# Attention and gated feed-forward on one core: batch 0's first layer and a third token tile of the second layer go from split to plain fp32 matmuls, in a new written-out order

## The chip, the core and the metric

The kernel runs on one core of a Trainium2 chip (trn2). The metric is the device time of one execution in microseconds, lower is better. The kernel before takes 394.97 us, the median of three runs (394.75 to 395.34).

## What is computed

Two blocks follow each other. The first is attention over a pack of 32 learned queries per head (8 batches, 8 heads, 576 tokens, 64 channels): the packed queries attend to k and v, and then q attends to the packed result. The second is a feed-forward block with a depthwise convolution of width 3 and a sigmoid gate.

```python
def sm_attn(qq, kk, vv):
    s = scale * np.matmul(qq, kk.transpose(0, 1, 3, 2))
    ...
    a = np.exp(s)
    a = a / (np.sum(a, axis=-1, keepdims=True) + 1e-09)
    return np.matmul(a, vv)
p_packed = sm_attn(p, k, v)
out = sm_attn(q, p_packed, p_packed)
...
h = np.maximum(x @ w_in, 0.0)
...
    conv_out += conv_w[k][None, None, :] * hp[:, k:k + S, :]
gate = 1.0 / (1.0 + np.exp(-conv_out))
return (h * gate @ w_out).astype(np.float32)
```

## The kernel before

**Tiling.** The attention runs in 16 groups of four heads, two groups for each batch. A group's softmax weights over the 32 packs end up transposed as a tile of 128 x 576 (`a2t`, line 940), that is 32 packs of four heads by 576 tokens. The packed values are not multiplied with these weights. They are folded into w_in first (`packed_weight`, lines 957 to 1018), so that the first layer of a batch is one product of the folded weights `gw` and the softmax weights `a2`.

**Split matmuls.** Both layers keep fp32 accuracy by splitting. An operand x becomes hi (a rounding cast to fp32r, a reduced format that TensorE takes in one go) and lo (x minus hi), and a product is three fp32r matmuls: hi with hi, lo with hi, hi with lo. For the softmax weights the cast is line 945 and the subtraction line 947. For the folded weights the cast is line 1006, and for batches 0 and 1 the remainder comes from TensorE, which subtracts hi from the bank with a matmul by minus the identity (line 1010), and a second cast (line 1015). For a tile of 128 tokens in front of the second layer these are `x` (line 1194) and `xl` (line 1201). The steps share the helper lines 334, 337, 342 and 344, so that in a profile one finds them by their tiles.

**First layer** (`ffn1`, line 1026). A batch has 8 chunks of 128 of the 1024 channels. Each is 12 matmuls of 288 columns (two groups, three products, two halves), then Relu, the three taps of the convolution, Tanh and the gate on ScalarE and VectorE.

**Second layer** (`ffn2`, line 1152). There are 36 tiles of 128 tokens. Each is 8 steps, and a step is three matmuls of 512 columns (line 1227). The first `F2F` tiles do without the split: a step is one plain fp32 matmul (line 1174) on w_out as loaded.

**What sets the order.** The kernel is a set of generators, one for each piece of work, and the string `ORDER` says by two characters at a time whose next step is emitted. Each engine works through its instructions in that order, and SyncE (SP) does the same with the loads. A planner in the same file (`Flow`) estimates when a TensorE step can start. As long as the second layer has not got to the tile behind those named in `SPLIT`, it puts matmuls on zeros (`warm`, line 288, here called fills) into gaps that it expects. They are real instructions of the program, whether the gap then is there or not.

**Switches.** `F1F` names batches whose first layer is plain fp32 (empty before), `F2F` the number of plain tiles of the second layer, `ON_DVE` and `ON_POOL` the steps that go to VectorE and GpSimd in place of their default engine.

```python
if g // NG in F1F:
    yield Step("DVE", 669, take=["a2"], give=["s2"], sets=[("hi", g), ("a2", g)])
    at = wk.tile([128, S], F32, name="a2f", tag="a2hi", bufs=4)
    nc.vector.transpose(out=at, in_=s2)
...
if b in F1F:
    ...
    copy(key, hi[:, :, n * p : n * p + n], t)
    gw[b, hf] = (hi,)
    continue
```

Of the kernel before, what the change touches and what calls it, by code (L numbers as in the profile page):

```python
# [18 lines left out]


ORDER = (
    "0036360336367f6y03026y36360736340504340501050a0504060a70060570346z053a0e05090805350c363405366z36340c0c34363b0505"
    "0d0h0h0572050c3b34050c7205053c050b0d05760l0b713b0j050c0c710j0c0c050j3d0c3b3q3q050c0c0k770c3d0c3d3q0o0o740k3q740g"
    "0c0c0i0j0c730i0j0c733d0c0q0c0q3e3f0q3q0f0c3q783s0j3g0r3q3f3f3s3s3s0j3f0j3i3q3t0m0n3h3k0j793s3h3h0j3t3s3t3u0j0r0q"
    "0j3u3s3j0q3t3h3r3t3j7a3v3r3v0q3u0p0q0p753r3j3u3j0q3v5y3t3u750q3v373r5z3l3t0s0q3w3v3m3u0j0q3r377b3w3l0j3u3l3w0q0j"
    "5z3w3x3l3r3j3x3r3v3r0j0q0v5y0j5z37403x3v0q0x3w3n0j5z5y400x0q400x3w0z3x7c3y0q5y3n403y3x0x3w3z3x3n0x3o0j0q0q0j3y12"
    "413z3n3x0j0t3p5y3y5y143p7d5z3y0u3p3z0q415z0q0x16143z0q143p3y413n3y3z3j425z5y413n3z3z424242435z3l155y440y60424314"
    "600y430x0x4244190w42433l445y3843603p601444456010434560154518115y43444544600x3p45464446465z45466045140x1461461b60"
    "46606061470x474748131b1d61461b0x49476161481b480x616149141g47616149471b6114484948140x481760494947484962140x4a6261"
    "4b1k0x0x1i4b631c1s1b0x611i1e621463621c3862141i1b621b621i1a0x1f621i0x1n381j1b624b0x621414621i1j1p1p1b6314634a1463"  # L30
    "1b146363631p631b63624a141i141p1b1i141q1r641h641l634c1u1b1y1p4c4c4d4d1i4e4d1b64641b4c1w4c4e1q1i4c4d4e4e4d1p4c641w"
    "4e1b4d1w644e65644d1b654f1p4f4g1i631p211m4g1b1w4f1p1w641o1i4k4k4g4f231p4e1w4f1p64644k4h4f4f4i641b251i1x4g4g1i1p4g"
    "651i4g1i6565651b1i1t1i2866656565234h4j1x4i4i4h651w1p23234j641w4l4j1w1v231i65661z391i244h2a1w23664i5z4j244i4j664h"
    "664j4j1w4l1p1i23664i664h2a2a6666231p4m1p4i4n4m661p4m4h67674l4o4n664m23681w4n1p2a4n6767674o2k6767671p67204m4n4o4m"
    "2a4m4p4o4n2c2b674p664n4q3967261w682a222f232b1w4q394p4o4u4q274q4o2a232j4o4q65692h2h694q2m1w681w4u1p4q4p68681w681p"
    "4r4p4r2h68684u682d68682i4s4p2h2a4s294r4s1w6969692a694p69232h4t4t2e68694t4s4r69694r2o1w4s4v4t6a6a2o692a2q2h1w6a2i"
    "4s4r6a2x2o4t4t4r6a6a4s4t236a2h2o6b2a236a6b1w2p236a6a69232h676a4w2o2a4x232t4w6b2h2a4w4y4v6c2p6b6b232l2g4w4w6b6b6b"
    "4y234w6b4x4w4z6b4x2v4z4y2z6b4y2a544v6c232h4x2o2v6d4y4z6c4x4x2v6c6a6c4z6c4z4x2h6c6c234y6c542v2h6c6d6c2h504y6b2a6d"
    "6e506d6d506d2h2a6d4z6d306d2r6e2w6c4z2n6d502w6d512v546f506e5051506e2o526e51516f2o516e6d6e53526e512h532o6e2a522a52"
    "6e2y532v32556e2h2a2h2o51522a6f2a6f52322h322v556f6f6f2o536e5356522o6f6f6f2h53565757536f6g58562v6g2o562h6g6g6g5758"  # L40
    "56576h576g6h566g562o6g586g6g58322o596g6h2o586h5755596h2s6i6g6h575a6h593258332v59585a5a6h6h59596i5a6h5b6j596h5a5a"
    "5b5c2o5c6i6i6j6i5b5a5d6i6i2o6i6h6i2h6i5d5c2u5b5e5c2v6i5f5b326j6j5b5d6j6j6j2o5e6f5d6j6j5c5d5d5c6i5b5e2o5d6j335f5c"
    "322v2o6k6k5g2v5f5h5g2v5g6j326k6l5i6k5h6k5i5g5h2v326k6k6k5h5h5h316k5i5h5j6k6k5g6l325j5i6k5j325o325j5j5j5i6l6l6l6l"
    "6l6l322v6l6m5j5o6m6l6l5i5g325k5k6j6n6m6m5o6m2v6m6m5g5k5i6m6m5l5l6m2v5m322v6n2v5k6m5k322v5l6n325k6n5k5m6n6m5m5l6n"
    "6o5n5m5m6o326n5n6n5n5n6n6l6n6n2v5l5l5p325n5n6o5m5l326o6n6o5n6o6o5m6p6o326o5p6o5q5q5r5s5r5p6o5q6p6p6p6p6p5q5r5q5s"
    "6p5q5s6q6p5q6p6p5t6q5s6p5t5s5r6q6q5t6r5s6o5t6q5r6q6q5t5s5r5t6q6q5u6r6q5t5r5u6s5u6q5v5w6r6r5u5v5u5u6r5u6r5w5v6s5w"
    "6r5v5w5x6r6p5x5v6r5w5x6r6s5w6s5v6r6s6s6s5x5x5x5w5v6s5x6s6t6s6t6t6u6r6t6t6s6t6t6t6u6t6t6u6u6s6v6v6t6u6u6u6u6u6u6w"
    "6v6v6v6t6v6u6v6v6w6v6v6q6w6u6w6w6w6w6v6w6w6w6x6x6x6x6v6x6x6x6x6x6x6w7e7e6x7e6w7e7e7e7e6x7e7e7e"
)


# [167 lines left out]
def tile_packed_attention_conv_gate(  # L219
# [79 lines left out]
    def early():  # L299
# [118 lines left out]
    def weight(i):  # L418
# [10 lines left out]
        if src.dtype != F32:  # L429
# [411 lines left out]
    def attention(g):  # L841
# [115 lines left out]
    def packed_weight(b, hf):  # L957
# [5 lines left out]
        for p in range(parts):  # L963
# [62 lines left out]
    def ffn1(b, j):  # L1026
# [125 lines left out]
    def ffn2(m):  # L1152
# [164 lines left out]
```

## Time and profile before

| what | value |
|---|---|
| median of 3 runs | 394.97 us |
| the profiled execution, its own time | 394.99 us |
| its span | 393.2 us |
| TensorE matmuls, busy | 386.5 us, 98% of the span |
| TensorE weight loads, busy | 310.8 us, 79% |
| VectorE | 334.5 us, 85% |
| ScalarE | 247.5 us, 63% |
| GpSimd | 72.6 us, 18% |
| mean granted clock of TensorE | 0.998 |

The span is the profiled part; 1.8 us of the execution's own time lie around it. A matmul's busy time holds its way through the array too, and neighbours overlap in it. What a matmul costs the engine is read from one start to the next. PE is TensorE, PEld its weight loads, DVE VectorE, ACT ScalarE, POOL GpSimd, SP SyncE. A plain fp32 matmul stands in the trace as two records, so that "x4" in a row of line 1174 is two steps.

### The profile page before, as it was taken

How to read it: one execution, taken by the hardware profiler on the slowest of the kernel's cores; microseconds unless marked ns; L12 is line 12 of the kernel's file. 1: busy time of each engine (PE TensorE's matmuls, PEld its weight loads, DVE VectorE, ACT ScalarE, POOL GpSimd, SP SyncE). 2: the span in 40 equal slices, each digit the busy share in tenths (PEclk: the TensorE clock that was granted, in tenths of full speed). 3: DMA queues.
4: the chain of work that ended last, by engine and by line, in shares of the span. 5: the costliest groups of instructions: out<-in, count | busy, mean ns of one | idle time of the engine just before them, and what ended most of it. 6: DMA issues, size and time to landing. Idle time of an engine off the chain costs nothing.

```text
span 393.2 us, 8191 instructions
## 1 busy us (share of the span) xinstructions
PE 386.5 (98%) x3300; PEld 310.8 (79%) x3300; DVE 334.5 (85%) x501; ACT 247.5 (63%) x405; POOL 72.6 (18%) x59
## 2 busy tenths in 40 slices
PE   8999999999999999999999999999999999999996
PEld 6667655789678787878797887888797879898886
DVE  4899999999989999999899989799988897987010
ACT  4799999987666776765746465564645555444211
POOL 2041134204441331052120103000001100200420
PEclk9999999999999999999999999999999999999999
DMA  8999799797499779578655134001001110000211
GB/s 268 367 374 363 161 263 156 144 187 147 99 175 168 127 171 152 120 149 162 129 81 140 43 87 88 1 28 53 28 2 53 41 41 27 28 0 28 80 54 56
DMA packets 157527, 47.63 MB, mean 121 GB/s; under 512 B 145444, under 2 KB 148772, under 8 KB 157488
## 3 DMA queue, kind: packets, MB, share of 16 engines
q1 hardware_dynamic: 157024, 45.89, 49.5%
q10 hardware_dynamic: 432, 1.18, 0.9%
q8 instruction: 26, 0.43, 0.5%
q14 instruction: 13, 0.11, 0.1%
q0 software_dynamic: 32, 0.02, 0.0%
HBM read 37.64 MB, written 9.44 MB: 120 GB/s over the span
## 4 chain that ended last, share of the span: by engine, by line
PE 89%; DMA 4%; DVE 3%; ACT 1%; issue 1%; SPq 1%; ACTq 0%; DVEq 0%
PE fo L1227 43%; PE big L1047 24%; PE sm L1227 4%; PE big L731 4%; PE big L1174 4%; PE big L982 3%; DMA hgt<-in_q_dram 3%; PE sm L876 2%; PE big L868 2%; DMA hgt<-in_k_dram 1%; PE fo L1133 1%; PE sm L1133 1%; ACT tmp L510 1%; PE big L711 0%; PE big L1010 0%
## 5 line engine op out<-in xcount | busy, mean ns | idle before, releaser
L1227 PE MATMUL fo<-wo_hi,xhi 128*128 128x512 f32 x240 | 96.5, 402 | 0.0
L1227 PE MATMUL fo<-wo_hi,xlo 128*128 128x512 f32 x240 | 94.0, 392 | 0.0
L1227 PE MATMUL fo<-wo_lo,xhi 128*128 128x512 f32 x240 | 93.6, 390 | 0.0
L1064 ACT ACTIVATE hbuf<-big 128x576 f32<-128x576 f32 x62 | 40.8, 659 | 52.7 <-PE big L1047 52.3
L1096 DVE SCALAR_TENSOR_TENSOR hgt<-hbuf,cw,hgt 128x576 f32<-128x576 f32 x64 | 53.4, 843 | 5.7 <-ACT hgt L1094 5.4
L1047 PE MATMUL big<-a2hi,ghi 128*128 128x288 f32 x256 | 57.0, 304 | 0.0
L1047 PE MATMUL big<-a2lo,ghi 128*128 128x288 f32 x256 | 54.9, 295 | 0.0
L1047 PE MATMUL big<-a2hi,glo 128*128 128x288 f32 x256 | 54.9, 295 | 0.0
L1227 PEld LDWEIGHTS fo<-wo_hi,xhi 128*128 128x128 f32 x240 | 45.0, 188 | 11.8 <-issue 0.9
L1104 ACT ACTIVATE hgt<-hgt 128x576 f32<-128x576 f32 x64 | 43.7, 693 | 16.6 <-DVE hgt L1100 16.5
L1227 PEld LDWEIGHTS fo<-wo_hi,xlo 128*128 128x128 f32 x240 | 45.0, 188 | 10.0
L1100 DVE SCALAR_TENSOR_TENSOR hgt<-hbuf,cw,hgt 128x576 f32<-128x576 f32 x64 | 51.2, 811 | 0.5
L1227 PEld LDWEIGHTS fo<-wo_lo,xhi 128*128 128x128 f32 x240 | 45.1, 188 | 7.4
L1106 DVE SCALAR_TENSOR_TENSOR hgt<-hgt,hbuf 128x576 f32<-128x576 f32 x64 | 47.5, 752 | 3.5 <-ACT hgt L1104 3.0
L1047 PEld LDWEIGHTS big<-a2hi,ghi 128*128 128x128 f32 x256 | 43.1, 189 | 6.9 <-issue 1.6
L337 POOL TENSOR_TENSOR xlo<-hgt,xhi 128x1024 fp32r<-128x1024 f32 x11 | 27.1, 2467 | 88.0 <-ACT xhi L344 57.2
L1047 PEld LDWEIGHTS big<-a2lo,ghi 128*128 128x128 f32 x256 | 41.1, 188 | 0.0
L1047 PEld LDWEIGHTS big<-a2hi,glo 128*128 128x128 f32 x256 | 41.0, 188 | 0.0
L1242 ACT COPY o<-fo 128x512 f32<-128x512 f32 x30 | 17.6, 585 | 34.8 <-PE fo L1227 26.8
L1094 ACT ACTIVATE hgt<-hbuf,cw 128x576 f32<-128x576 f32 x42 | 32.8, 788 | 2.6 <-DVE hbuf L1062 2.0
L344 ACT CAST xhi<-hgt 128x1024 fp32r<-128x1024 f32 (+1 forms) x29 | 27.6, 956 | 8.9 <-PE fo L1227 4.0
L337 POOL TENSOR_TENSOR s<-s,mx 128x576 f32<-128x576 f32 x10 | 13.0, 1300 | 100.0 <-DVE hgt L1100 67.2
(127 smaller groups left out, 593.4 us busy)
## 6 DMA issues: line engine op xcount, KB each, us to landing
out_dram<-o SPq DMA_DIRECT2D x35, 256.0 KB, 2.2
k<-in_k_dram SPq DMA_DIRECT2D x48, 144.0 KB, 3.3
q<-in_q_dram SPq DMA_DIRECT2D x48, 144.0 KB, 3.1
v<-in_v_dram SPq DMA_DIRECT2D x40, 128.0 KB, 3.0
v<-in_v_dram SPq DMA_DIRECT2D x6, 512.0 KB, 9.7
hgt<-in_moe_w_in_dram SPq DMA_DIRECT2D x3, 1024.0 KB, 12.0
hgt<-in_moe_w_out_dram SPq DMA_DIRECT2D x3, 1024.0 KB, 6.8
k<-in_k_dram SPq DMA_DIRECT2D x2, 576.0 KB, 10.5
```

The lines of the kernel that those rows point to most:

```text
L337: added = nc.gpsimd.tensor_tensor(**kw)
L344: nc.scalar.copy(out=out, in_=in_)
L731: nc.tensor.matmul(out=o.rearrange("c (j r) -> c j r", r=NR) if by_block(g) else o, lhsT=lhs[r, 32 * cols[i] : 32 * cols[i] + 32], rhs=rhs ...
L1047: nc.tensor.matmul(out=t[:, hf, :SH], lhsT=w[:, gg, js], rhs=x[:, hf * SH : (hf + 1) * SH], start=n == 0, stop=n == (1 if b in F1F else 3) ...
L1064: nc.scalar.activation(out=inner, in_=t[:, :, :SH], func=AF.Relu, scale=0.5)
L1094: nc.scalar.activation(out=d, in_=h[:, 1 : S + 1], func=AF.Copy, scale=cw[:, NJ + j : NJ + j + 1])
L1096: nc.vector.scalar_tensor_tensor(out=d, in0=h[:, 0:S], scalar=cw[:, j : j + 1], in1=d, op0=ALU.mult, op1=ALU.add)
L1100: nc.vector.scalar_tensor_tensor(out=d, in0=h[:, 2 : S + 2], scalar=cw[:, 2 * NJ + j : 2 * NJ + j + 1], in1=d, op0=ALU.mult, op1=ALU.add)
L1104: nc.scalar.activation(out=d, in_=d, func=AF.Tanh)
L1106: nc.vector.scalar_tensor_tensor(out=d, in0=d, scalar=1.0, in1=h[:, 1 : S + 1], op0=ALU.add, op1=ALU.mult)
L1227: nc.tensor.matmul(out=t, lhsT=x[:, c, :], rhs=w[:, c % 2, :], start=c + i == 0, stop=c == NJ - 1 and i == 2)
L1242: nc.scalar.copy(out=o, in_=t)
```

## The change

Batch 0 goes into `F1F` and `F2F` goes from 2 to 3. Batch 0's two groups then no longer cast and subtract their transposed softmax weights, its four folded weight pieces are only copied (no remainder, no matmul by minus the identity), and a chunk of its first layer is 4 plain fp32 matmuls of 288 columns in place of 12 split ones. Token tile 2 of the second layer is 8 plain matmuls in place of 24 split ones and needs no cast and no subtraction of its tokens. `ORDER` is new up to about a third of its length and the same behind it, and some steps have another engine.

```diff
 ORDER = (
-    "0036360336367f6y03026y36360736340504340501050a0504060a70060570346z053a0e05090805350c363405366z36340c0c34363b0505"
...
+    "00367f3603360e6y073602033634366y36050a0536360570060105700434340a0c063a05040h340c0h050c6z056z3472363605090508723b"
...
 )
...
-    ON_DVE = {"gh001", "gh510", "gl000", "hi0", "hi12", "kT10", "relu34", "relu76", "tap00", "tap02", "tap22", "tap40", ...
-    ON_POOL = {"add00", "add10", "add11", "add30", "add50", "add60", "add70", "lo0", "lo10", "lo11", "lo4", "lo6", "lo7", ...
+    ON_DVE = {"a1T1", "gh510", "hi12", "kT00", "kT10", "kT20", "relu34", "relu76", "tap01", "tap03", "tap21", "tap40", ...
+    ON_POOL = {"add01", "add10", "add31", "add40", "add41", "add50", "add51", "add60", "add70", "add71", "lo10", "lo11", "lo7", ...
     COLD = 7
-    F1F = ()
-    F2F = 2
+    F1F = (0,)
+    F2F = 3
```

Over the whole program TensorE loses 96 split matmuls of the first layer, 24 of the second, 8 matmuls by minus the identity and one fill (24 in place of 25), and gains 32 plain matmuls of 288 columns and 8 of 512. VectorE has as many instructions as before (503), ScalarE 7 fewer, GpSimd 3 fewer, SP as many. The last 1377 matmuls are the same, in the same order.

TensorE around the start of the first layer, before. `a2hi`, `a2lo`, `ghi` and `glo` are the split softmax weights and folded weights, `idle` a fill, line 982 the folding, line 1010 the matmul by minus the identity:

```order
L291 MATMUL idle<-zeros 128x512 x4
L982 MATMUL big<-w_in_sb,ppT 32x256 x8
L1047 MATMUL big<-a2hi,ghi 128x288 x2
L1047 MATMUL big<-a2lo,ghi 128x288 x2
L1047 MATMUL big<-a2hi,glo 128x288 x2
...
L876 MATMUL sm<-v_88,a1T 32x64 x20
L1010 MATMUL big<-ghi,minus 128x256 x2
```

The same place in the change. `a2f` and `gwf` are the unsplit operands:

```order
L711 MATMUL big<-ident,q 128x128 x9
L731 MATMUL big<-kT,pT 32x288 x8
L291 MATMUL idle<-zeros 128x512 x4
L1047 MATMUL big<-a2f,gwf 128x288 x8
L982 MATMUL big<-w_in_sb,ppT 32x256 x8
L876 MATMUL sm<-v_88,a1T 32x64 x20
```

The second folding now stands behind the first two chunks, and the matmuls by minus the identity are gone. Ahead of the first matmul of line 1047 everything else on TensorE is there as often as before, fills included (24).

SP at the start of the program, one piece of the difference. Lines 643 are loads of k and q (`hgt_75<-in_k_dram` is group 1's keys, `k<-in_k_dram` those of groups 2 and 3), 603 and 613 of v, 411 of weights:

```order
 L788 DMA stage<-in_p_dram 32x16x64
+L643 DMA k<-in_k_dram 128x1152
 L643 DMA hgt_75<-in_k_dram 128x1152
 L603 DMA v_88<-in_v_dram 128x4x256
 L613 DMA v_88<-in_v_dram 64x4x64
 L411 DMA hgt_76<-in_moe_w_in_dram 128x4x512
-L643 DMA k<-in_k_dram 128x1152
 L643 DMA hgt_75<-in_q_dram 128x1152
 L603 DMA v_89<-in_v_dram 128x4x256
 L613 DMA v_89<-in_v_dram 64x4x64
```

Group 2's keys now go ahead of group 1's; what is loaded up to group 1's values (`v_89`) is the same.

SP further on, another piece of the difference, around the third and fourth block of w_out:

```order
-L652 DMA k<-in_k_dram 32x36x32 x4
-L411 DMA hgt_76<-in_moe_w_out_dram 128x2x1024
-L652 DMA k<-in_k_dram 32x36x32 x4
+L652 DMA k<-in_k_dram 32x36x32 x8
 L411 DMA hgt_76<-in_moe_w_out_dram 128x2x1024
```

The third block of w_out now stands behind eight loads of keys, not four.

## Rows read from the trace of the kernel before

**Rows 1.** The page, parts 1 and 4: busy time by engine; the chain's shares.
```profile
PE 386.5 (98%) x3300; PEld 310.8 (79%) x3300; DVE 334.5 (85%) x501; ACT 247.5 (63%) x405; POOL 72.6 (18%) x59
...
PE 89%; DMA 4%; DVE 3%; ACT 1%; issue 1%; SPq 1%; ACTq 0%; DVEq 0%
```

**Rows 2.** Busy time in stretches of 10 us, granted clock, DMA share, GB/s.
```profile
20.00:30.00 10.00, 9.71 (x139) 6.25 (x127) 9.40 (x18) 9.26 (x17) 5.29 (x4) 1.00 1.06 372
30.00:40.00 10.00, 9.86 (x139) 7.61 (x138) 9.19 (x17) 10.00 (x17) 1.30 (x1) 1.00 1.06 352
40.00:50.00 10.00, 9.81 (x116) 6.52 (x115) 10.00 (x16) 10.00 (x18) 2.15 (x2) 1.00 0.79 179
50.00:60.00 10.00, 9.99 (x70) 5.35 (x68) 10.00 (x18) 10.00 (x16) 3.95 (x4) 1.00 1.06 247
```

**Rows 3.** Who waited, TensorE, whole span: us in total, times, longest.
```profile
PE big L711 <- DMA hgt<-in_k_dram: 0.6, 1, 0.6
PE big L711 <- DMA hgt<-in_q_dram: 0.6, 1, 0.6
PE big L711 <- ACT hbuf L1064: 0.2, 1, 0.2
```

**Rows 4.** Timeline of TensorE up to batch 0's first chunk: start, us, then the group.
```profile
20.20 0.77 PE L876 MATMUL sm<-v,a1T 128*32 128x64 f32 x40
...
24.40 0.50 PE L1010 MATMUL big<-ghi,minus 128*128 128x256 f32 x2
24.74 1.15 PE L711 MATMUL big<-ident,k 128*128 128x128 f32 x9
...
29.05 1.19 PE L291 MATMUL idle<-zeros 128*128 128x512 f32 x4
30.18 0.66 PE L982 MATMUL big<-w_in_sb,ppT 64*32 64x256 f32 x16
30.77 0.53 PE L1047 MATMUL big<-a2hi,ghi 128*128 128x288 f32 x2
...
32.55 0.77 PE L876 MATMUL sm<-v,a1T 128*32 128x64 f32 x40
```

**Rows 5.** Timeline of VectorE: group 1's last transpose, and its neighbours.
```profile
25.96 0.67 DVE L342 CAST glo<-big 128x512 fp32r<-128x512 f32 x1
...
28.70 0.78 DVE L940 STREAM_TRANSPOSE a2t<-s 128x576 f32<-128x576 f32 x1
...
30.21 0.76 DVE L334 TENSOR_TENSOR a2lo<-a2t,a2hi 128x576 fp32r<-128x576 f32 x1
```

**Rows 6.** Timeline of TensorE: starts of a split chunk and of split steps.
```profile
157.22 0.43 PE L1047 MATMUL big<-a2hi,ghi 128*128 128x288 f32 x2
...
158.82 0.40 PE L1227 MATMUL fo<-wo_hi,xhi 128*128 128x512 f32 x1
...
161.57 0.48 PE L1227 MATMUL fo<-wo_hi,xhi 128*128 128x512 f32 x1
...
166.45 0.43 PE L1047 MATMUL big<-a2hi,ghi 128*128 128x288 f32 x2
```

**Rows 7.** Timeline of TensorE: plain fp32 steps and a matmul by minus the identity.
```profile
51.21 0.40 PE L1010 MATMUL big<-ghi,minus 128*128 128x256 f32 x2
51.44 1.88 PE L1174 MATMUL big<-w,hgt 128*128 128x512 f32 x4
53.25 1.09 PE L982 MATMUL big<-w_in_sb,ppT 64*32 64x512 f32 x16
...
59.10 1.03 PE L1174 MATMUL big<-w,hgt 128*128 128x512 f32 x2
59.97 0.81 PE L868 MATMUL big<-ident,a 128*128 128x128 f32 x5
...
63.29 1.98 PE L1174 MATMUL big<-tmp,hgt 128*128 128x512 f32 x4
```

**Rows 8.** Timeline of SP's issues: the third block of w_out, then four loads of keys.
```profile
45.13 0.87 SPq L411 DMA_DIRECT2D hgt<-in_moe_w_out_dram  x1
46.10 6.37 SPq L652 DMA_DIRECT2D k<-in_k_dram  x4
```

More of the change, by code (lines that the diff above doesn't have):

```diff
@@ L21 @@
 ORDER = (
-    "0036360336367f6y03026y36360736340504340501050a0504060a70060570346z053a0e05090805350c363405366z36340c0c34363b0505"
[L23 to L46, printed above, removed]
@@ L47 @@
-    "6r5v5w5x6r6p5x5v6r5w5x6r6s5w6s5v6r6s6s6s5x5x5x5w5v6s5x6s6t6s6t6t6u6r6t6t6s6t6t6t6u6t6t6u6u6s6v6v6t6u6u6u6u6u6u6w"
-    "6v6v6v6t6v6u6v6v6w6v6v6q6w6u6w6w6w6w6v6w6w6w6x6x6x6x6v6x6x6x6x6x6x6w7e7e6x7e6w7e7e7e7e6x7e7e7e"
+    "00367f3603360e6y073602033634366y36050a0536360570060105700434340a0c063a05040h340c0h050c6z056z3472363605090508723b"
+    "0c34050d0l0j760c05340d0b05710b3c3b053b05050j0g71350c0c0c053b05050o0c0c0j0o0j0c3q0j3d0c740c0c050i740k0c0c733q0c0c"
+    "3e0q0c0i77733f3d3d783s3s0q3s0q3f0f3g3t0k3d3f3s0r3q0m3s3t3i3t3q0j3f0r0j0q3s0n0j3u3h0j0q3t793s0j373u0q3t3h3r3h0q3h"
@@ new lines @@
+    "3v3t0j0q3r3u3j3v0j3k0p3t0j757a750q3w0s3u0p3v3r403u3u3v3j3v3w3r0q3u3j3w3v3x0j40373l0q3v3j0j0q0j3w3y7b3l3x603y3w3x"
+    "40375y0q3w0v0z5z0j3w0j400x3l0x3m0t600q3z0j3l0x0j0x123y3z3z3n0q3y0x0q0j3z0y5y5y5y7c3n0q3o603y3z0q16413j3n140u1441"
+    "3z0x3y5z0y5z415z0q0q143z3x3p7d3n603x3x410q603p3y5z3j3x3p1019420x5y424342423l0x3l42184343435z4244141d60151443423p"
+    "5y430w154443453n445y4660450x14453n440x46451b11445y45605z4644454661443p17455z46460x611b1g600x460x471b4748495y6013"
+    "4748470x3p4714491e6149140x48471b1b49616138481449485z6161494761494861611b481c5y0x621c0x14141b621k61631i4a4b1i1b62"
@@ new lines @@
+    "0x63141b62621i1a1i62380x624a621i5z611r62141f621i1n4a381j14141b1j14621b0x140x1b141p631p63631i631b4b6363631l1p1m14"
+    "641p634b141i1q141u631b644c1b4c1h4d1i63644c4c1q1b4d4c1s4e4d4d4c644e4c4d1p64644e4d1y1p4e4e4e654d1w1i4f1b1b1i1w1w4f"
+    "1i644g1p4e4h1x4g1i1p1w65641o1x4f1i211i6464231w1p1b4h4f4f4g234k644f1p4f254h4h664g231b4h1i1w4k641b1w4k1i654g1i6265"
+    "4h4i6565654h23664g1w651p1t651i1z23654j281w651i1i1p1v4i664i4i4j664g4i231w1p4j4i2a1w4l2a2a664m4i1p4n4j4j654j1p6666"
+    "4m664j66664o4n1w4m666724671p2a244m68391p671p4n1p23674n674o2k23674l2a6767674m4l4m204m4o4n4p4o232c2b4n66674p4n4q67"
@@ new lines @@
+    "1w262a68391w222f232b4q394p4o4u4q274q4o2j4o234q2a692h2h694q2m1w684u1p4q4p6868681w1p4r4p4r1w2h68684u682d68682i4s4p"
+    "2h4s294r4s2a691w6969692a4p692h234t4t2e68694t4s4r69694r2o1w4s4v4t6a6a2o2a692q2h1w6a2i4s4r6a2x2o4t4t4r6a6a4s4t236a"
+    "2h2o6b2a236a6b1w2p236a6a69232h676a4w2o2a4x232t4w6b2h2a4w4y4v6c2p6b6b232l2g4w4w6b6b6b4y234w6b4x4w4z6b4x2v4z4y2z6b"
+    "4y2a544v6c232h4x2o2v6d4y4z6c4x4x2v6c6a6c4z6c4z4x2h6c6c234y6c542v2h6c6d6c2h504y6b2a6d6e506d6d506d2h2a6d4z6d306d2r"
+    "6e2w6c4z2n6d502w6d512v546f506e5051506e2o526e51516f2o516e6d6e53526e512h532o6e2a522a526e2y532v32556e2h2a2h2o51522a"
@@ new lines @@
+    "6f2a6f52322h322v556f6f6f2o536e5356522o6f6f6f2h53565757536f6g58562v6g2o562h6g6g6g575856576h576g6h566g562o6g586g6g"
+    "58322o596g6h2o586h5755596h2s6i6g6h575a6h593258332v59585a5a6h6h59596i5a6h5b6j596h5a5a5b5c2o5c6i6i6j6i5b5a5d6i6i2o"
+    "6i6h6i2h6i5d5c2u5b5e5c2v6i5f5b326j6j5b5d6j6j6j2o5e6f5d6j6j5c5d5d5c6i5b5e2o5d6j335f5c322v2o6k6k5g2v5f5h5g2v5g6j32"
+    "6k6l5i6k5h6k5i5g5h2v326k6k6k5h5h5h316k5i5h5j6k6k5g6l325j5i6k5j325o325j5j5j5i6l6l6l6l6l6l322v6l6m5j5o6m6l6l5i5g32"
+    "5k5k6j6n6m6m5o6m2v6m6m5g5k5i6m6m5l5l6m2v5m322v6n2v5k6m5k322v5l6n325k6n5k5m6n6m5m5l6n6o5n5m5m6o326n5n6n5n5n6n6l6n"
@@ L49 @@
+    "6n2v5l5l5p325n5n6o5m5l326o6n6o5n6o6o5m6p6o326o5p6o5q5q5r5s5r5p6o5q6p6p6p6p6p5q5r5q5s6p5q5s6q6p5q6p6p5t6q5s6p5t5s"
+    "5r6q6q5t6r5s6o5t6q5r6q6q5t5s5r5t6q6q5u6r6q5t5r5u6s5u6q5v5w6r6r5u5v5u5u6r5u6r5w5v6s5w6r5v5w5x6r6p5x5v6r5w5x6r6s5w"
+    "6s5v6r6s6s6s5x5x5x5w5v6s5x6s6t6s6t6t6u6r6t6t6s6t6t6t6u6t6t6u6u6s6v6v6t6u6u6u6u6u6u6w6v6v6v6t6v6u6v6v6w6v6v6q6w6u"
+    "6w6w6w6w6v6w6w6w6x6x6x6x6v6x6x6x6x6x6x6w7e7e6x7e6w7e7e7e7e6x7e7e7e"
 )
@@ L251, in tile_packed_attention_conv_gate @@
     PE_LO = 2
-    ON_DVE = {"gh001", "gh510", "gl000", "hi0", "hi12", "kT10", "relu34", "relu76", "tap00", "tap02", "tap22", "tap40", "tap41", "tap42", "tap44", "tap46", "tap53", "tap56", "tap57", "tap60", "tap61", "tap64", "tap65", "tap67", "tap70", "tap72", "tap73", "tap74", "tap75", "tap77", "x140", "x180", "x230", "x270", "x280", "x310", "x340", "x90"}
-    ON_POOL = {"add00", "add10", "add11", "add30", "add50", "add60", "add70", "lo0", "lo10", "lo11", "lo4", "lo6", "lo7", "mul10", "mul12", "mul14", "mul2", "mul3", "mul4", "mul5", "mul6", "mul7", "mul9", "sub10", "sub11", "sub15", "sub2", "sub3", "sub4", "sub5", "sub6", "sub8", "sub9", "xl100", "xl110", "xl20", "xl280", "xl30", "xl320", "xl330", "xl350", "xl50", "xl60", "xl70"}
+    ON_DVE = {"a1T1", "gh510", "hi12", "kT00", "kT10", "kT20", "relu34", "relu76", "tap01", "tap03", "tap21", "tap40", "tap41", "tap42", "tap44", "tap46", "tap53", "tap56", "tap57", "tap60", "tap61", "tap64", "tap65", "tap67", "tap70", "tap72", "tap73", "tap74", "tap75", "tap77", "x140", "x180", "x230", "x270", "x280", "x310", "x340", "x90"}
+    ON_POOL = {"add01", "add10", "add31", "add40", "add41", "add50", "add51", "add60", "add70", "add71", "lo10", "lo11", "lo7", "mul0", "mul10", "mul12", "mul14", "mul4", "mul5", "mul6", "mul9", "sub10", "sub11", "sub15", "sub3", "sub4", "sub5", "sub7", "sub8", "sub9", "xl100", "xl110", "xl280", "xl30", "xl320", "xl330", "xl350", "xl50", "xl60", "xl70", "xl80"}
     COLD = 7
-    F1F = ()
-    F2F = 2
+    F1F = (0,)
+    F2F = 3
     SPLIT = (0,1)
```

## The prediction

> **What bounds the kernel now.** I read the page first, then the stretches of 10 us, TensorE's waits, and then the timeline of TensorE from start to start. TensorE's matmuls cover 98% of the span, and the chain that ended last lies on it for 89% [rows 1]. That alone is weak, because fills count as busy and neighbouring matmuls overlap. The waits say more: besides the wait for the first memset, the profile knows three idle stretches of TensorE in the whole run, 0.6, 0.6 and 0.2 us [rows 3]. Fills cover most of what else was lost, and the program has 25 of them. All but one stand ahead of batch 0's first layer, which begins at 30.77 us [rows 4]. Behind that there is always real work for TensorE, at the full granted clock: it is busy 9.99 of 10 us from 50 to 60 us, while VectorE and ScalarE are busy for 10.00 of 10 as well [rows 2]. So I read two regimes. Up to about 30 us TensorE waits for loads and for the attention's chain over VectorE and ScalarE; from there to the end, the time is the sum of what TensorE has to do. The change removes work mostly from ScalarE and adds work to TensorE, and most of it lies in the second regime.
>
> **First layer of batch 0.** A split chunk in steady state runs from 157.22 to 158.82 us: 1.60 us for 12 matmuls [rows 6]. The chunk at the start took 1.78 us, 30.77 to 32.55, because it follows other kinds of matmul [rows 4]; the new chunks have the same neighbours, so I compare without that. A plain fp32 matmul of 288 columns is not in the trace. The nearest is one of 512 columns: 0.87 us (59.10 to 59.97), and 0.905 us as the mean of the two between 51.44 and 53.25 [rows 7]. By columns 288 take 0.49 to 0.51 us, so a chunk of four takes 1.96 to 2.04 us. The gain is then 0.36 to 0.44 us a chunk, or as little as 0.18 if the whole 1.78 us were the split chunk's own. I take 0.36, since the 0.905 includes a change of kind: 8 x 0.36 = **+2.9 us** (1.4 to 3.5).
>
> **Third token tile.** A split step costs 4.88 / 7 = 0.70 us (161.57 to 166.45, seven steps [rows 6]), a plain one 0.87 to 0.905 [rows 7]. 8 x 0.17 = **+1.4 us** (to 1.6).
>
> **Matmuls by minus the identity.** Four pairs go. One pair held TensorE from 24.40 to 24.74, 0.34 us [rows 4], another for 0.23 us, 51.21 to 51.44 [rows 7]. I take 0.34: **-1.4 us** (-0.9 to -1.4). **One fill fewer**: four took 1.13 us (29.05 to 30.18 [rows 4]), so **-0.3 us**.
>
> **Start of the first layer.** Ahead of its first matmul TensorE has the same work and the same 24 fills as before, except one folding of 0.59 us (30.18 to 30.77) and one of the pairs, 0.34 us [rows 4]. With the same lost time it starts at 30.77 - 0.93 = 29.84 us, and nothing is won beyond the pair already counted, as the folding only moves behind the first two chunks. Can the chain be earlier? Group 1's transpose ended at 28.70 + 0.78 = 29.48 us [rows 5]. The split then still had to cast and subtract (the subtraction began at 30.21 [rows 5]); without it, the two matmuls of group 0 (0.98 us) can run ahead of group 1's, so an unchanged chain would allow a start at 28.5 plus a handover of 0.2, that is 28.7. That would win 1.1 us. Against it stand the loads. Up to group 1's values SP loads the same bytes as before, so the step that multiplies with them (20.20 us [rows 4]) is hardly earlier, and the new order has eight fills right ahead of it, which run even when the values are there. At 372 GB/s [rows 2] the 590 KB of group 2's keys put group 1's keys back by 1.6 us, and TensorE already waited 0.6 us for these [rows 3]. That extra wait is covered as long as group 1's queries come no later, for which TensorE waited 0.6 us too [rows 3]; without that cover it costs up to 1.6 us. I take **0** (-1.1 to +1.6).
>
> **What costs nothing.** The casts and subtractions of group 0 and 1's weights, of the folded weights and of tile 2 go from ScalarE, VectorE and GpSimd, and the moves between `ON_DVE` and `ON_POOL` give VectorE about as much back (503 instructions, as before). All of it lies beside TensorE's work; the wait of 0.2 us for ScalarE [rows 3] is the only one that it could end, and I leave it in the range. On SP the third block of w_out is now behind eight loads of keys, so it is issued up to 6.4 us later than at 45.13 [rows 8]. It was first used at 63.29 us [rows 7], 18.2 us after its issue; at the same pace it is ready at 69.7. By the two lists of TensorE's instructions, with the durations above, about 10 us more of TensorE's work stand ahead of that matmul than before, which puts it near 73. That slack is the cover.
>
> **Sum.** 2.9 + 1.4 - 1.4 - 0.3 + 0 = +2.6. Against the profiled execution's 394.99 us (the median is 394.97, so nothing has to be moved) that gives **397.6 us**.
>
> **Rivals.**
>
> *The start comes earlier.* The chain allows 28.7 us, and the fills are placed for that: 397.6 - 1.1 = 396.5. For it: the cast of a remainder at 25.96 us (0.67) stood between group 1's steps on VectorE [rows 5] and is gone. Against it: the eight fills. Chance 0.16.
>
> *Faster: ScalarE and VectorE are what holds the start.* Between 20.20 us and 29.48 us group 1 goes through a chain of 9.3 us [rows 4, 5] in which VectorE and ScalarE are busy for 9.4 and 9.3 of 10 us [rows 2]. With the casts gone the chain could close up, and weights and first taps come sooner. To be faster by more than 0.2 us, about what a measurement can tell from no change here, the first layer has to start more than 2.8 us before 29.84, at 27.0 or earlier. The chain would have to lose 1.7 us of its 9.3; the one cast seen inside it is 0.67 us. With 2 us lost it would start at 26.7, and the time would be 397.6 - 3.1 = 394.5 (within no change), with 2.5 us lost 394.0. The Trainium skill, Perfetto Trace Analysis, "Identifying the Most-Contended Engine", speaks for this rival: it says that matmul busy time is a poor measure for TensorE while occupancy is a fair one for the others, so that by its rule ScalarE and VectorE at 10.00 of 10 are the ones to relieve from 40 to 60 us. The trace differs there: only 0.2 us of TensorE's waits name ScalarE. Chance 0.06 for faster, and 0.07 for a start so much earlier that nothing is left either way.
>
> *A plain matmul costs four of the split's.* A split matmul of 288 columns takes 1.60 / 12 = 0.133 us, one of 512 takes 0.233 [rows 6]. At four each, a chunk is 2.13 us and a step 0.93: 8 x 0.53 + 8 x 0.23 = 6.1 instead of 4.3, and 399.4 us. The rows of line 1174 speak against it: 0.87 to 0.905 is less than 0.93, though none has 288 columns. The Trainium skill, FP8 and Floating Point Precision, "TensorE Precision Notes", has fp32 as four passes, which by its count is this rival's 4 against 3; the trace shows 0.87 / 0.70, nearer to 3.7 against 3. Chance 0.08.
>
> *New waits.* Keys of group 1 not covered (+1.6), or weights and gates late for the plain steps of the second layer, for which the fills stop once its third tile has begun: 1 to 3 us more, 398.6 to 400.6. For it: three loads stand later on SP, and VectorE and ScalarE are full from 40 to 60 us [rows 2]. Against it: the slack above. Chance 0.15.
>
> **How the numbers follow.** My forecast, the sum with its bounds, has 0.48. It is 397.6, itself 396.9 to 398.6. The range goes from 395.9, which takes in most of the earlier start, to 400.2, which takes in the four passes and most of the new waits; it leaves out the two cases with no loss (0.13) and a rest of the last rival. Faster 0.06, within 0.2% (394.2 to 395.8) 0.09, slower 0.85.
>
> **What would show it.** Right: line 1047 with `gwf` at 0.49 us from start to start, line 1174 at 0.87 in all three tiles, the first layer's start between 29 and 30.4 us, no wait of TensorE over 0.5 us behind it, the last 1377 matmuls as before but 2 to 3 us later. Wrong: a start at 27 us or earlier, or idle time of TensorE between 45 and 75 us that names w_out, ScalarE or VectorE.

## The result, and the profile after

The changed kernel takes 397.52 us, the median of 9 runs (395.69 to 398.68), where the kernel before took 395.0 us in the runs beside it (9 runs, 394.44 to 395.5). The ratio is 1.006, with a 95% interval from 1.005 to 1.0071: slower, by 2.5 us. The forecast was 397.6 us. The profiled execution took 397.36 us with a span of 395.6 us, 2.4 us longer than before.

The value is right, but the trace shows that it is right for a reason that I did not give. The start of the first layer came 1.75 us later than forecast, and the work behind it cost some 2.0 us less.

The page after, busy time by engine, then TensorE's tenths and granted clock in 40 slices, then the chain's shares:

```profile
PE 388.3 (98%) x3251; PEld 309.8 (78%) x3251; DVE 335.5 (85%) x501; ACT 243.0 (61%) x398; POOL 70.9 (18%) x56
...
PE   7999999999999999999999999999999999999996
...
PEclk9899999999999999999999999999999999999999
...
PE 88%; ACT 6%; DVE 3%; DMA 2%; issue 1%; SPq 0%; DVEq 0%; ACTq 0%
```

ScalarE lost 4.5 us of work and TensorE's busy time grew by 1.8 us [rows 1]. The 8 in the second slice of the granted clock is the one thing here that points at the surprise. The waits of TensorE in the changed kernel name the place:

```profile
PE big L711 <- DMA hgt<-in_k_dram: 2.3, 1, 2.3
PE idle L302 <- DVE stage L278: 1.1, 1, 1.1
```

The second row is the wait for the first memset, as before. The first is group 1's keys: 2.3 us in one piece, where before it was 0.6 [rows 3]. The 0.6 us for group 1's queries is gone. Behind that, the profile knows no wait of TensorE at all.

TensorE's timeline in the changed kernel, start in us, duration, then the group:

```profile
7.62 0.72 PE L731 MATMUL big<-kT,pT 64*32 64x288 f32 x16
...
10.64 2.15 PE L711 MATMUL big<-ident,hgt 128*128 128x128 f32 x9 [2.30 <-DMA hgt<-in_k_dram]
12.45 1.20 PE L291 MATMUL idle<-zeros 128*128 128x512 f32 x2
...
19.85 1.20 PE L711 MATMUL big<-ident,hgt 128*128 128x128 f32 x9
20.81 2.09 PE L291 MATMUL idle<-zeros 128*128 128x512 f32 x8
22.83 0.77 PE L876 MATMUL sm<-v,a1T 128*32 128x64 f32 x40
...
31.59 4.04 PE L1047 MATMUL big<-a2f,gwf 128*128 128x288 f32 x16
35.56 0.66 PE L982 MATMUL big<-w_in_sb,ppT 64*32 64x256 f32 x16
```

Three things stand here. The nine transposes of group 1's keys (line 711 at 10.64) held TensorE for 1.81 us, to 12.45, while the nine of the queries at 19.85 took 0.96. The queries' transposes have no wait in their row: the load that before came 0.6 us late was now there first, so it covered nothing. And the step on group 1's values (line 876) begins at 22.83, not at 20.20 [rows 4]. The first layer begins at 31.59 us, where the forecast had 29.84 and before had 30.77 [rows 4].

Why the transposes were slow stands in the short stretches of the changed kernel (busy time of TensorE, its weight loads, VectorE, ScalarE and GpSimd, granted clock, DMA share, GB/s):

```profile
10.00:11.00 1.00, 0.36 (x2) 0.39 (x3) 0.27 (x2) 0.06 (x1) 0.00 (x0) 0.67 1.11 372
11.00:12.00 1.00, 1.00 (x7) 1.00 (x6) 0.02 (x1) 0.00 (x0) 0.00 (x0) 0.50 1.14 280
12.00:13.00 1.00, 1.00 (x5) 0.93 (x4) 0.87 (x2) 0.11 (x1) 0.00 (x0) 0.50 1.03 317
13.00:14.00 1.00, 1.00 (x6) 0.77 (x5) 0.21 (x1) 0.90 (x3) 0.00 (x0) 0.63 1.06 393
14.00:15.00 1.00, 1.00 (x16) 0.80 (x23) 0.00 (x0) 0.65 (x2) 0.00 (x0) 1.00 1.05 402
```

In the 2.3 us of idling the granted clock fell to 0.50, the lower of its two levels, and it stayed there until between 13 and 14 us. The means of 0.67 and 0.63 in the first and the fourth row place the fall at about 10.3 us and the rise at about 13.7. So the late load cost its wait and then half of TensorE's pace for some 3.1 us of work, from 10.64 on.

The other runs of the change bear on this too. The mean granted clock of the whole execution was 0.994 to 0.996 in eight of the nine (397.36 to 398.68 us), and 1.000 in the ninth, which took 395.69 us. That one has no profile, so where it won its time is not shown; but the loss of the clock does not come with every execution.

Further on, TensorE's timeline in the changed kernel shows a single plain chunk, a pair by minus the identity and plain steps:

```profile
37.65 2.11 PE L1047 MATMUL big<-a2f,gwf 128*128 128x288 f32 x8
39.69 0.71 PE L731 MATMUL big<-qT,ppT 64*32 64x288 f32 x16
...
67.63 1.02 PE L1010 MATMUL big<-ghi,minus 128*128 128x512 f32 x2
68.49 1.02 PE L1174 MATMUL big<-w,hgt 128*128 128x512 f32 x2
69.35 1.02 PE L1174 MATMUL fo<-w,hgt 128*128 128x512 f32 x2
70.21 1.02 PE L1174 MATMUL fo<-tmp,hgt 128*128 128x512 f32 x2
71.07 1.02 PE L1174 MATMUL big<-tmp,hgt 128*128 128x512 f32 x2
```

Two chunks from 31.59 to 35.56 are 1.985 us each, or 0.496 us a matmul. A single one, 37.65 to 39.69, is 2.04. Plain steps of 512 columns that follow each other are 0.86 us apart.

### The profile page after: what moved, and what is told of

Read it like the earlier page. It is cut to its first block, busy times and chain, and to the rows that moved or that the text cites. A ratio compares the mean times of both kernels' runs of the same rounds, so it can differ in the third digit from the quotient of the medians.

```text
span 395.6 us, 8074 instructions
## 1 busy us (share of the span) xinstructions
PE 388.3 (98%) x3251; PEld 309.8 (78%) x3251; DVE 335.5 (85%) x501; ACT 243.0 (61%) x398; POOL 70.9 (18%) x56
## 4 chain that ended last, share of the span: by engine, by line
PE 88%; ACT 6%; DVE 3%; DMA 2%; issue 1%; SPq 0%; DVEq 0%; ACTq 0%
PE fo L1227 41%; PE big L1047 23%; PE sm L1227 4%; PE big L731 4%; PE big L1174 3%; PE big L982 3%; DMA hgt<-in_k_dram 2%; PE sm L876 2%; PE big L868 2%; PE fo L1174 2%; PE big L711 1%; ACT tmp L448 1%; ACT tmp L510 1%; PE fo L1133 1%; PE sm L1133 1%; ACT hbuf L1064 1%
## 5 line engine op out<-in xcount | busy, mean ns | idle before, releaser
L1227 PE MATMUL fo<-wo_hi,xhi 128*128 128x512 f32 x232 | 93.2, 402 | 0.0
L1227 PE MATMUL fo<-wo_hi,xlo 128*128 128x512 f32 x232 | 90.9, 392 | 0.0
L1227 PE MATMUL fo<-wo_lo,xhi 128*128 128x512 f32 x232 | 90.5, 390 | 0.0
L1227 PEld LDWEIGHTS fo<-wo_hi,xhi 128*128 128x128 f32 x232 | 43.6, 188 | 11.6 <-issue 1.8
L1047 PE MATMUL big<-a2hi,ghi 128*128 128x288 f32 x224 | 50.8, 308 | 0.0
L1047 PE MATMUL big<-a2lo,ghi 128*128 128x288 f32 x224 | 48.1, 296 | 0.0
L1047 PE MATMUL big<-a2hi,glo 128*128 128x288 f32 x224 | 48.0, 295 | 0.0
L1047 PEld LDWEIGHTS big<-a2hi,ghi 128*128 128x128 f32 x224 | 38.1, 189 | 6.4 <-issue 2.6
L1047 PEld LDWEIGHTS big<-a2lo,ghi 128*128 128x128 f32 x224 | 36.0, 189 | 0.0
L1047 PEld LDWEIGHTS big<-a2hi,glo 128*128 128x128 f32 x224 | 35.9, 189 | 0.0
```

The lines of the kernel that those rows point to most:

```text
L1047: nc.tensor.matmul(out=t[:, hf, :SH], lhsT=w[:, gg, js], rhs=x[:, hf * SH : (hf + 1) * SH], start=n == 0, stop=n == (1 if b in F1F else 3) ...
L1227: nc.tensor.matmul(out=t, lhsT=x[:, c, :], rhs=w[:, c % 2, :], start=c + i == 0, stop=c == NJ - 1 and i == 2)
```

## Experiments

All kernels were timed in five rounds against the kernel before. "Start" below is the start of batch 0's first layer on TensorE, read from the timeline: 30.77 us before, 31.59 in the change, 29.84 forecast.

### Group 1's keys loaded first again

The change with two entries of `ORDER` exchanged: `02` loads group 1's keys, `0e` those of groups 2 and 3.

```diff
-    "00367f3603360e6y073602033634366y...
+    "00367f360336026y07360e033634366y...
```

> The change, with group 1's keys loaded ahead of group 2's again, as before (23 fills ahead of the first layer instead of 24). Theory A (late keys): the 2.3 us wait for group 1's keys and the half clock behind it are what made the first layer start at 31.59 us; without them it starts at 29.3 to 30.3 and the time falls by 1.3 to 2.2 us, to 395.3 to 396.2. Theory B (cover): the loads of queries and values and the eight fills hold the start anyway; it stays above 31 us and the time at 397.0 or more.

Measured: 394.68 us, median of 11 (394.17 to 395.82), ratio 0.9986 (0.9975 to 0.9997), span 393.3. That is 2.8 us less than the change by the medians and 2.3 by the spans. TensorE's timeline in this kernel:

```profile
8.84 1.17 PE L711 MATMUL big<-ident,hgt 128*128 128x128 f32 x9 [0.49 <-DMA hgt<-in_k_dram]
9.77 0.48 PE L291 MATMUL idle<-zeros 128*128 128x512 f32 x1
...
17.60 1.18 PE L711 MATMUL big<-ident,hgt 128*128 128x128 f32 x9 [0.81 <-DMA hgt<-in_q_dram]
18.53 2.10 PE L291 MATMUL idle<-zeros 128*128 128x512 f32 x8
20.55 0.77 PE L876 MATMUL sm<-v,a1T 128*32 128x64 f32 x40
...
29.31 3.07 PE L1047 MATMUL big<-a2f,gwf 128*128 128x288 f32 x12
```

The keys' transposes begin 1.8 us sooner (8.84 for 10.64) and take 0.93 us instead of 1.81. The lead is 2.25 us at the queries' transposes and 2.28 at the start of the first layer (29.31 for 31.59), and it is still 2.3 us in the span. So the load order alone makes the change slower than the kernel before. The rest of the change costs nothing that shows, 393.3 against 393.2 us of span, and that is a sum of two: the first layer starts 1.46 us sooner than in the kernel before (29.31 for 30.77), and the work behind it takes as much longer. The start is what theory A expected; the time is 0.6 us below its 395.3 to 396.2.

### Fills in the wait for the keys

The change, with ten fills emitted between group 0's scores and the transposes of group 1's keys. The loads stay as late as they are.

```diff
             t = score(G["pT"], G["kT"], g, heads)
+        if g == 0:
+            warm(10)
         yield Step("DVE", 665)
```

> The change with ten more fills right behind group 0's scores, that is in the wait for group 1's late keys. The loads are untouched. Theory clock: of the 2.3 us that the late keys cost, more than half is the granted clock that falls in the wait (the nine transposes behind it took 1.81 us, against 0.9 at the full clock). With fills in the wait it does not fall, the first layer starts 1.0 to 1.6 us earlier, 30.0 to 30.6, and the time is 396.0 to 396.6. Theory wait: the wait itself is the cost; start and time stay within 0.3 us, 397.2 to 397.8.

Measured: 396.05 us (9 runs), ratio 1.0025 (1.0016 to 1.0035), span 394.2. TensorE's timeline in this kernel:

```profile
8.35 2.61 PE L291 MATMUL idle<-zeros 128*128 128x512 f32 x10
10.79 1.15 PE L711 MATMUL big<-ident,hgt 128*128 128x128 f32 x9
11.69 0.71 PE L291 MATMUL idle<-zeros 128*128 128x512 f32 x2
...
30.26 4.04 PE L1049 MATMUL big<-a2f,gwf 128*128 128x288 f32 x16
```

and its stretch from 11 to 12 us:

```profile
11.00:12.00 1.00, 1.00 (x10) 0.97 (x9) 0.46 (x1) 0.00 (x0) 0.00 (x0) 1.00 1.13 311
```

The transposes begin even later than in the change (10.79 for 10.64), and yet they are done 0.76 us sooner, because the granted clock stayed at 1.00: 0.90 us instead of 1.81. The start is 30.26, 1.33 us sooner, and the span is 1.4 us shorter. Of the 2.28 us that the late keys cost, 1.33 hang on the clock, and 0.95 (30.26 against 29.31) on the wait itself, some 0.15 of them on fills that ran past the moment at which the keys' transposes began in the change.

### The same load order in the kernel before

The kernel before with only its `0e` moved directly ahead of `07`. The planner puts five fills into the gap by itself.

```diff
-    "...7f6y03026y36360736...3a0e05...
+    "...7f6y03026y36360e0736...3a05...
```

> The kernel before with group 2's keys ahead of group 1's, as in the change; here the planner puts five fills into the wait. Theory clock: the keys come 1.6 us later, but the clock stays up and group 1's queries are waited for behind it, so 0.2 to 0.9 us slower, 395.4 to 396.1. Theory wait: the loads' order costs the same in any order, 2 us or more slower, 397.1 or more.

Measured: 396.24 us (10 runs), ratio 1.0036 (1.0022 to 1.0049), span 394.4. TensorE's timeline in this kernel:

```profile
8.30 1.40 PE L291 MATMUL idle<-zeros 128*128 128x512 f32 x5
10.57 0.77 PE L711 MATMUL big<-ident,hgt 128*128 128x128 f32 x5 [0.88 <-DMA hgt<-in_k_dram]
```

The keys come as late as in the change (10.57), the idling is 0.9 us and not 2.3, and the granted clock stays at 1.00 in this profile. The cost is 1.1 us by the medians and 1.2 by the spans, the start 32.06 for 30.77. That is above the 0.2 to 0.9 us that I expected for a wait without a loss of clock, and far from the 2 us and more of the change. It bears out the share of 0.95 us for the wait alone, which I had put too low.

### Two fills instead of eight ahead of group 1's values

The kernel with the keys first, with the planner held to two fills at that place.

```diff
-        while self.matmuls(at, ...) + self.MARGIN <= until:
+        most = 2 if ("s2", 0) in self.done and ("s2", 1) not in self.done else 99
+        while n < most and self.matmuls(at, ...) + self.MARGIN <= until:
```

> The change with its keys put back, and two fills in place of eight ahead of group 1's values. These landed at about 19.9 us there, the eight fills ended at 20.55. Theory fills: the start moves by 0.4 to 0.6 us, from 29.31 to 28.7 to 28.9, and the time is 394.1 to 394.3. Theory chain: the steps behind it wait for ScalarE and VectorE anyway; start and time stay, 394.6 to 394.8.

Measured: 394.45 us (11 runs), ratio 0.9989 (0.9977 to 1.0), span 392.6. TensorE's timeline in this kernel:

```profile
18.97 0.77 PE L877 MATMUL sm<-v,a1T 128*32 128x64 f32 x40 [0.31 <-DMA v<-in_v_dram]
...
21.07 0.33 PE L900 MATMUL sm<-ident,pb 128*128 128x128 f32 x1 [0.90 <-ACT pb L890]
...
28.58 2.59 PE L1048 MATMUL big<-a2f,gwf 128*128 128x288 f32 x10
```

With six fills gone the values' step begins 1.6 us sooner, at its load. Half of the gain is lost at once to ScalarE, for which TensorE now waits 0.9 us. The start comes 0.73 us sooner and the span is 0.7 us shorter; the medians differ by only 0.2 us, and the ratios to the kernel before are 0.9989 and 0.9986, which can't be told from no difference. Two of the eleven runs had a mean granted clock of 0.995 and 0.996 and took 396.0 and 396.28 us, the others 394.13 to 394.70. So the eight fills did hold TensorE where the values were there, as the forecast said of them, but what they held back was worth 0.7 us and not 1.6. The start is past the 28.7 to 28.9 of theory fills, and the time lies between the two theories.

### The plain first layer alone, in the old order

The kernel before with batch 0 in `F1F` and the steps that this drops taken out of `ORDER` (two `05`, two `0c`, four `3q`, four `3r`).

```diff
-    F1F = ()
+    F1F = (0,)
```

> The kernel before with batch 0's first layer in plain fp32 alone, in the order of before (27 fills instead of 25). Theory A (dear neighbours): next to other kinds of matmul a split chunk costs 1.74 us and a plain one 2.01, so 8 x 0.27 = 2.2, less 1.5 for the matmuls by minus the identity: 0.5 to 1.0 us slower, 395.5 to 396.0. Theory B (as predicted): 2.9 - 1.4 = 1.5 us slower, 396.4 to 396.7. Theory C (the start was held by ScalarE and VectorE): faster than 394.5.

Measured: 396.94 us (5 runs), ratio 1.0043 (1.003 to 1.0055), span 394.9, start 30.96. It costs 1.6 us by the medians, the 1.5 us that the forecast's terms give. The pieces are not those of the forecast, though. TensorE's timeline in this kernel:

```profile
28.78 1.66 PE L291 MATMUL idle<-zeros 128*128 128x512 f32 x6
30.37 0.66 PE L982 MATMUL big<-w_in_sb,ppT 64*32 64x256 f32 x16
30.96 2.21 PE L1047 MATMUL big<-a2f,gwf 128*128 128x288 f32 x8
33.10 0.77 PE L876 MATMUL sm<-v,a1T 128*32 128x64 f32 x40
```

Six fills stand ahead of the folding, where before there were four [rows 4]; I read this as the planner filling what the missing matmuls by minus the identity leave. 27 fills in all, two more than before, are worth about 0.6 us (at the 0.28 each of rows 4). The 32 plain matmuls held TensorE for 16.4 us here, start to start, 2.05 a chunk, where the split chunks had taken 1.74 (see "First layer" below). 8 x 0.31 = 2.5, less 1.5 for the matmuls by minus the identity, plus 0.6, is the 1.6.

### The third tile alone, in the old order

The kernel before with `F2F = 3`, and the tile's eight steps (`60`) each right behind one of tile 1 (`5z`).

```diff
-    F2F = 2
+    F2F = 3
```

> The kernel before with the third token tile in plain fp32 alone, its steps right behind the second tile's, otherwise the order of before. TensorE alone counts: 8 x (0.86 - 0.70) = 1.3 us slower, 396.1 to 396.5. Rival (changes of kind): plain steps next to plain steps save what a change of kind costs, and it is 0.3 to 0.9 us slower. Rival (the freed cast and subtraction let TensorE start other work earlier): no slower than 395.2.

Measured: 400.29 us (4 runs), ratio 1.0125 (1.0112 to 1.0139), span 397.9. It costs 5 us, for a change that the forecast prices at 1.4, and it misses all three expectations. The waits of TensorE in this kernel (us in total, times, longest) hold 3.6 us that before did not have:

```profile
PE big L1047 <- DVE s L910: 1.5, 1, 1.5
PE sm L876 <- ACT ppT L902: 1.1, 1, 1.1
...
PE big L1047 <- ACT a1T L344: 1.0, 1, 1.0
```

They lie between 86 and 95 us. In the kernel before, the 24 split matmuls of this tile stood in that stretch of the program (77.86 to 88.70 us there), and TensorE had them to do while batch 2's attention went through ScalarE and VectorE. Taken away from there, they leave TensorE waiting. The rest, 5.0 - 3.6 = 1.4 us, is as much as the forecast has for the tile itself; no run measures it alone.

### The third tile as late as the old order allows

To see whether only the place of the steps was at fault, the same switch with the eight steps about as late as the old order allows: four, two and two of them, each group directly ahead of the step that takes the low part of a block of w_out. Six of the eight still stand ahead of the place in `ORDER` at which the split steps of this tile had begun.

```diff
+ ORDER: 60 60 60 60 ahead of 3j 42; 60 60 ahead of 3n 3z; 60 60 ahead of 3p 45
```

> The kernel before with the third token tile in plain fp32 alone, as in the third experiment, but its steps as late as that order allows: each just ahead of the step that takes the low part of its block of w_out. Theory place (the 3.6 us of waits between 80 and 100 us there came because the tile's steps were used up early): less is lost, 396.0 to 398.0, and the waits of TensorE behind 60 us are under 2 us in all. Theory price (a plain third tile costs 5 us wherever it stands): 399.5 to 400.5 again.

Measured: 399.52 us (5 runs), ratio 1.0113 (1.0097 to 1.0129), span 397.7. Theory place missed: 4.5 us of cost, nearly as much as before. Two of the three waits remain, together 2.1 us where under 2 was expected (TensorE's waits in this kernel):

```profile
PE big L1047 <- DVE s L910: 1.5, 1, 1.5
...
PE sm L876 <- ACT ppT L902: 0.6, 1, 0.6
```

Eight plain steps are less work than the 24 split matmuls that had filled this stretch, and the steps could not go further back without moving others. What of the 4.5 us is place and what is the number of steps stays open.

### Both switches in the old order

The two edits above together: batch 0 in `F1F`, and `F2F = 3` with the steps behind tile 1's.

> The kernel before with both switches, in the order of before, without the new order. If the parts add up: 395.0 + 0.7 + 1.3 = 396.7 to 397.3 by theory A, 397.6 to 398.0 by theory B. If the new order is worth something beside its late keys, this is slower than the change with its keys put back; if not, it is the same or faster.

Measured: 402.46 us (5 runs), ratio 1.0182 (1.0168 to 1.0196), span 400.6. That is 7.1 us over the kernel before, close to 1.6 + 5.0, and 4.5 us over the highest value expected. The same arithmetic on TensorE takes 394.68 us in the new order with the keys first, so that the new order, together with the steps that have another engine in it, is worth 7.8 us to these two switches.

### The new order with a split first layer

The kernel with the keys first, with batch 0 split again, the dropped steps put back, and its casts on the engines of before.

```diff
-    F1F = (0,)
+    F1F = ()
```

> The change with its keys put back, but batch 0's first layer split again, each cast and remainder right behind the step that it belongs to; third tile plain. Theory order needs the switch: casts and remainders stand in front of other steps on ScalarE, VectorE and TensorE in this order, and TensorE waits (the planner puts in 57 fills in place of 23): slower than 394.7 by 4 to 9 us, 399 to 404. Theory sum of TensorE's work: the plain first layer costs 1.1 us more than it saves, so without it 393.3 to 394.0.

Measured: 405.06 us (4 runs), ratio 1.0252 (1.0235 to 1.0269), span 402.9, start 32.83. The fills of this kernel (count, busy us, mean ns), and its stretch from 60 to 70 us:

```profile
L291 PE MATMUL idle<-zeros 128*128 128x512 f32 x64 | 17.8, 407 | 0.0
```
```profile
60.00:70.00 10.00, 8.92 (x48) 4.83 (x47) 10.00 (x18) 8.51 (x14) 4.14 (x3) 1.00 0.99 188
```

That is 10.4 us over the kernel with the keys first, and 1.1 us over the 399 to 404 expected. 64 fills stand in it where the kernel with the keys first has 23: the planner expects more and longer gaps, and puts in 41 more. From 60 to 70 us VectorE is busy for 10.00 of 10 and TensorE for 8.92. The same stretch of the change:

```profile
60.00:70.00 10.00, 10.00 (x96) 4.91 (x95) 10.00 (x20) 9.97 (x15) 1.64 (x1) 1.00 1.05 163
```

VectorE is as full there, and TensorE is busy for 10.00, so a full VectorE alone does not make TensorE wait. Fills run whether or not the gap is there, as the run with two of them showed, so how much of the 10.4 us are real waits and how much are the 41 fills is open; and the casts were put back in one way only. What the two runs show is that the new order loses its worth with the casts put back like this, and that the switches cost 7.1 us in the old order. Neither part of the change can be priced alone and added.

## Why the prediction was right, point by point

**The value** was right by two errors of opposite sign. From the split step below on, TensorE's rows are the same in the kernel before, in the change and in the kernel with the keys first (in this order):

```profile
163.73 0.39 PE L1227 MATMUL fo<-wo_hi,xhi 128*128 128x512 f32 x1
166.00 0.48 PE L1227 MATMUL fo<-wo_hi,xhi 128*128 128x512 f32 x1
163.72 0.48 PE L1227 MATMUL fo<-wo_hi,xhi 128*128 128x512 f32 x1
```

To this point the change loses 2.3 us, against 2.6 forecast. Up to the first layer's start it loses 0.8 where I had -0.9, and behind the start 1.5 where I had +3.5: 2.9 and 1.4, less 1.1 for the three pairs and 0.3 for the fill behind it, and 0.6 for the folding that moves there. That the two errors cancel is luck.

**Start of the first layer: "I take 0 (-1.1 to +1.6)".** This failed. The mechanism stood in the same paragraph: the keys put back by 590 KB, and a cover that holds "as long as group 1's queries come no later". I judged that cover by the 0.6 us that TensorE had waited for the queries, and even by these figures 1.6 us on a wait of 0.6 leave 1.0. The runs show two faults. The delay has to be weighed against the whole cover: 1.8 us of later start, 0.9 us of slower transposes and 0.65 us more for the fills behind them (1.00 us to the next step for 0.35), on 0.8 us of wait for the queries and 0.3 us of small gaps that were there to absorb it. And I priced the wait as a wait only. The trace shows that the granted clock fell with it, and the run with ten fills in the gap shows that this was 1.33 of the 2.28 us. Without the late keys the start is 29.31, so that 29.84 was itself 0.5 us too late (0.3 of it is one fill fewer in that kernel): the rival of an earlier start was half right.

**First layer, +2.9.** The sign and the price of a plain matmul were right: 0.496 us for 288 columns, inside 0.49 to 0.51. The whole group of 32 held TensorE for 16.11 us, start to start, 2.01 a chunk. What failed is "the new chunks have the same neighbours, so I compare without that". The eight split chunks of batch 0 in the kernel before took 1.78 us on average there, start to start, not 1.60. One of them, 1.97 us at 49.24, holds some 0.3 us of the plain step in front of it; without that the average is 1.74. One of the others, from 33.97 to 35.74 us:

```profile
33.97 0.51 PE L1047 MATMUL big<-a2hi,ghi 128*128 128x288 f32 x2
...
35.74 0.71 PE L731 MATMUL big<-qT,ppT 64*32 64x288 f32 x16
```

By these rows a split chunk between other kinds of matmul loses about 0.15 us, while a plain one loses 0.05 (2.04 alone, 1.985 in a pair). The term is +2.2 us.

**Third tile, +1.4.** A plain step by itself was right: 0.86 us where I had 0.87 to 0.905, against 0.73 for the eight split ones of this tile in the kernel before. But TensorE's plain steps and all split matmuls but batch 0's chunks, start to start up to the common point, together grew from 87.1 to 87.5 us, and by 0.1 us only if the 0.3 us above are counted to their plain step. In the new order the steps stand up to four in a row (from 68.49 us on, above), and before they stood in ones and twos between other kinds, 0.96 each at 63.29 [rows 7]. I read the missing 0.9 us (8 x 0.13 less 0.1) as fewer changes of kind. No run tests that by itself.

**Matmuls by minus the identity, -1.4.** Batch 0's four pairs had taken 0.34, 0.64, 0.32 and 0.24 us in the kernel before, 1.54 in all, and they are gone. Batch 1's two large ones became dearer (0.73 and 0.57 to 0.86 each, as between 67.63 and 68.49 us), so that 0.4 is given back. **One fill fewer**: 0.3 us, as taken.

**What costs nothing.** The cover of w_out's third block held: TensorE waits for nothing behind the first layer's start, and the plain steps run at their pace. It was thinner than I had it, though. The last step that readies the block on VectorE, in the change:

```profile
68.64 0.70 DVE L334 CUSTOM_DVE_ANT_0 tmp<-tmp 128x1024 uint16<-128x1024 uint16 x1
```

It ended at 69.34 us, near the 69.7 forecast, but TensorE's first matmul on the block began at 70.21 and not near 73, so that the block as a whole was ready only 0.9 us ahead. The rows asked for under "What would show it" are all there but one, the start between 29 and 30.4 us.

**The rivals.** Four passes at the price of a split matmul each fell: 0.496 us is 3.7 times the split's 0.133, a chunk 1.99 and not 2.13, and a step 0.86 and not 0.93. The Trainium skill, FP8 and Floating Point Precision, "TensorE Precision Notes", counts four passes for fp32; by these rows that holds roughly, as 3.7. The new wait for group 1's keys is what happened, with a cost of 2.3 us where I had 1.6, and I had given its rival 0.15. The relief of ScalarE and VectorE shows in no wait of the kernel before. It may be worth something in the new order, which has 64 fills with the casts of batch 0 put back and 23 without; no run prices it.

**A version that beats the change.** With group 1's keys first the kernel takes 394.68 us, ratio 0.9986 (0.9975 to 0.9997), and with two fills at the values 394.45, ratio 0.9989 (0.9977 to 1.0). Both are under the change by 0.7%, and under the kernel before by about 0.1%, too little to call them faster than that.

## What to carry to other kernels

When loads on one queue change places, follow the late one to the next wait that could absorb it, and check that this wait still exists after the change; then ask what the engine's clock does in the gap. A forecast that comes out right should be checked at an intermediate point of the program, here the start of the first layer: that point was off by 1.75 us while the end was off by 0.1. Work that fills an engine's gaps has a value beyond its own duration, so a cheaper version of it, or one in another place, can cost several times its own price (the third tile: 1.4 us of matmuls by the forecast, 5.0 us of time in the old order).

## What the runs showed of the hardware

In an idle stretch of TensorE of 2.3 us (8.34 to 10.64) the granted clock fell to 0.50 and stayed there to about 13.7 us, and nine transposes then took 1.81 us instead of 0.93. In the profiles with five fills and 0.9 us of idling in the same place, and with ten fills and none, it stayed at 1.00. A late load at the start of a kernel therefore cost 2.3 us where the wait itself was worth 0.95, and ten matmuls on zeros in the gap bought 1.33 us of that back.

The loss of the clock differs from run to run of one program. By the mean granted clock, one of the nine runs of the change kept it (1.000, 395.69 us). With five fills one of ten runs had 0.996 and took 398.77 us, where the median was 396.24. With ten fills it was 0.998 or more in all nine. The runs that have no profile do not show where they lost it.
